# Late exponentials, skip terms as matmul products in PSUM, and PSUM leaving through ScalarE

## The chip, the cores and the metric

The kernel runs on one core of one Trainium2 chip. The metric is the device time of the core in microseconds (us), as the median of several executions. Engines are named as in the profile: PE is TensorE (matrix products), DVE is VectorE, ACT is ScalarE, POOL is GpSimd, SP is SyncE (it issues most transfers).

## The reference, cut to what matters

The kernel computes a sum of three parts over 2048 tokens of 576 channels, and the gradients of all their inputs. The cut version:

```python
xn = layernorm(x)
out = x + ssm_conv(xn, A, B, C, log_dt, Dskip) + ffn(xn, W_gate, W_up, W_down)
# ssm_conv: K[d, l] = Re sum_n C * exp(dt*A*l) * dt*B ;  y = causal_conv(xn, K) + xn * Dskip
# ffn:      (relu(xn @ W_gate) * (xn @ W_up)) @ W_down
# returned: out, and the gradients of x and of all weights for a given grad_out
```

Two places matter. The decay `exp(dt*A*l)` is built from factors that are exponentials of `dt * A_re` times a small set of exponents. And the skip terms `xn * Dskip` (forward) and `grad_out * Dskip` (backward) are added to the two outputs in the last part of the kernel.

## The kernel before

The feed-forward work (matrix products, 11 full chunks of it and a final one) runs the whole time on PE. The transform work of the convolution is cut into small steps, which a greedy scheduler puts between those products when the program is built: every step yields a weight, and the order of all instructions on all engines follows from the weights and from estimates of time. So the order within an engine's queue is fixed at build time.

The final chunk goes through 16 tiles of 128 tokens. For each, PE sums in PSUM the inverse transform of the convolution, the residual, the earlier chunks' sum and the last chunk's products. VectorE has made the skip product `f_base` before, and adds it to PSUM (line 1043):

```python
class Final:
    def load(self, t):
        ...
        self.pool = pool("fin3", 3)                      # at t == 0: three buffers of everything
        ...
        xg = self.pool.tile([P, 2, D], BF16, name="f_xg")
        nc.sync.dma_start(xg[:, 0, :], g.xn_dram[:, t, :])
        nc.sync.dma_start(xg[:, 1, :], g.g_v[:, t, :])
        ...
        base = self.pool.tile([P, 2, D], F32, name="f_base")
        nc.vector.tensor_tensor(base[:], xg[:], self.dsk[:]...to_broadcast([P, 2, D]), op=ALU.mult)   # L1024
        return S3, Ct, xt, xg, acc, base
    def begin(self, t):
        for n in range(t, min(t + 3, ST)):               # loads three tiles ahead
            if n not in self.parts:
                self.parts[n] = self.load(n)
        ...
    def take(self, t, i, cols, ps):                      # four times per tile
        base = self.parts[t][5]
        dst = self.o[:, 0, cols] if i == 0 else base[:, 1, cols]
        self.g.nc.vector.tensor_tensor(dst, base[:, i, cols], ps, op=ALU.add)                         # L1043
    def end(self, t):                                    # gradient of the layer norm
        nc.scalar.activation(acc[:, 1, :], dx, ACT.Copy, accum_out=m[:, 0:1])
        nc.vector.scalar_tensor_tensor(acc[:, 0, :], dx, 1.0, xn, ..., accum_out=m[:, 1:2])           # L1055
        ... # two small ones, one more pass, one activation, one addition, two transfers out
```

The exponentials are made early, in 18 double steps, and written to HBM, from where two halves (each half of the channels) of the transform `p2(0)` and `p2(1)` read them:

```python
def ex_step(i):
    ex = exp_.tile([P, 2 * SX, NE], F32, name="exs")
    v.tensor_tensor(ex[:], pw[:, 0, i*SX:(i+2)*SX]..., self.ev[:]..., op=ALU.mult)
    nc.scalar.activation(ex[:], ex[:], ACT.Exp)
    nc.sync.dma_start(self.ex_dram[:, i:i + 2], ...)
...
yield from self.both(self.p1(0, 4, 10.0), 68.0, self.params(pw), 45.0)      # params holds all ex_steps
with ExitStack() as c:
    pools = self.p2_pools(c)
    yield from self.both(self.p2(0, pools, pw), 0.8 * W2, self.p1(1, 2, 3.0), W1)
    yield from self.both(self.p2(1, pools, pw), 0.8 * W2, self.p3(0, 2, 3.0), W3)
yield from self.p3(1, 4, 8.0)
```

Of the kernel before, what the change touches and what calls it, by code (L numbers as in the profile page):

```python
# [2 lines left out]

# [11 lines left out]
P = 128  # L15
# [141 lines left out]
class Ffn:  # L157
# [110 lines left out]
    def outdx(self, c, sg, j, last=None, turns=()):  # L268
        g, nc = self.g, self.g.nc
        t = sg * JS + j  # L270
        js = slice(j * P, (j + 1) * P)
        if last is None:
            o = self.op.tile([P, 2, D], BF16, name="osx")
        else:
            last.begin(t)
        src = self.t_steps(turns)
        Ts = [self.T[(c, sg, ft)] for ft in range(FTC)]
        for which in range(2):
            for hf in range(2):
                hs = slice(hf * DH, (hf + 1) * DH)  # L280
                if which == 0:
                    mms = [(Ts[ft][0], self.wf[:, 0, ft, hs]) for ft in range(FTC)]
                else:
                    mms = [(Ts[ft][1], self.wf[:, 1, ft, hs]) for ft in range(FTC)] + [(Ts[ft][2], self.wf[:, 2, ft, hs]) for ft in range(FTC)]
                mms = [(lt[:, js], rh) for lt, rh in mms]
                if last is not None:
                    mms = last.terms(t, which, hf) + mms
                ps = g.psum_mm.tile([P, 512], F32, name="ps_mm")
                for i, (lt, rh) in enumerate(mms):
                    nc.tensor.matmul(ps[:, :DH], lhsT=lt, rhs=rh, start=(i == 0), stop=(i == len(mms) - 1))  # L290
                if last is None:
                    g.bal.copy(o[:, which, hs], ps[:, :DH], DH)
                else:
                    last.take(t, which, hs, ps[:, :DH])
                next(src, None)
            if which == 0:
                yield FTC * 0.245
        if last is not None:
            last.end(t)
        elif c == 0:  # L300
            nc.gpsimd.dma_start(g.acc_dram[:, t, :, :], o[:])
        else:
            nc.gpsimd.dma_start(g.acc_dram[:, t, :, :], o[:], accum_op=ALU.add)  # L303
        yield FTC * 0.49
# [155 lines left out]
class S4:  # L460
# [84 lines left out]
    def params(self, pw):  # L545
        g, nc, bal = self.g, self.g.nc, self.g.bal
        v = nc.vector
        with ExitStack() as c:
# [14 lines left out]

            def ex_step(i):
                shp = [P, 2 * SX, NE]
                ex = exp_.tile(shp, F32, name="exs")
                v.tensor_tensor(ex[:], pw[:, 0, i * SX:(i + 2) * SX].unsqueeze(2).to_broadcast(shp), self.ev[:].unsqueeze(1).to_broadcast(shp), op=ALU.mult)
                nc.scalar.activation(ex[:], ex[:], ACT.Exp)
                nc.sync.dma_start(self.ex_dram[:, i:i + 2], ex[:].rearrange("p (i d) e -> p i d e", d=SX))
                bal.add(d=1.4, a=1.2)  # L570

            for i in range(0, 8, 2):
                ex_step(i)
                yield 2.0
            p1 = pool.tile([P, D], F32, name="p1")
            p2 = pool.tile([P, D], F32, name="p2")
            v.scalar_tensor_tensor(pw[:, 1, :], Ai, 1.0 / TWO_PI, dt[:], op0=ALU.mult, op1=ALU.mult)
            for j, (y1, y2, op) in enumerate(((Br, Bi, ALU.subtract), (Bi, Br, ALU.add))):
# [5 lines left out]
                yield 2.0  # L584
            for i in range(8, D // SX, 2):
                ex_step(i)
                yield 2.0

# [29 lines left out]
    def mix(self, dst, src):  # L618
        g, nc = self.g, self.g.nc
        for o in range(2):  # L620
            ps = self.ps()
            for i in range(2):
                nc.tensor.matmul(ps[i * 64:(i + 1) * 64, :DH], lhsT=self.FM[:, o, :], rhs=src[:, i, :], start=True, stop=True)
            g.bal.copy(dst[:, o, :], ps[:, :DH], DH)
            if o == 0:
                yield 0.15

# [35 lines left out]
    def p1(self, hf, n, gap):  # L663
# [11 lines left out]
        with ExitStack() as c:  # L675
# [10 lines left out]
            for h in range(ST + 1):  # L686
                old, Z = Z, None
                if h < ST:
                    b = bs.get(h)
                    if h == 0:  # L690
                        yield gap
                    sg = fp.tile([P, 2, 2, DH], BF16, name="s_ug")
                    for i in range(2):
                        yield from self.mix(sg[:, i], b[:, :, i, :])
                        yield 0.15
                    nc.sync.dma_start(self.S[hf][h], sg[:])
                    Z = self.product(fp, pp, sg[:, 1], sg[:, 0], True)
                    yield 0.7
# [27 lines left out]
    def p3(self, hf, n, gap):  # L726
# [13 lines left out]
        with ExitStack() as c:  # L740
# [13 lines left out]
            for h in range(ST + 1):  # L754
                old, Z = Z, None
                if h < ST:
                    b, sg = bs.get(h)
                    if h == 0:
                        yield gap
                    sk = fp.tile([P, 2, DH], BF16, name="s_k")  # L760
                    yield from self.mix(sk[:], b[:, :, 0, :])
                    Z = self.product(zp, pp, sg[:, 0], sk[:], False), self.product(zp, pp, sg[:, 1], sk[:], True)
                    yield 0.7
# [213 lines left out]
    def gen(self):  # L977
# [4 lines left out]
        with ExitStack() as cp:  # L982
# [9 lines left out]
            with ExitStack() as c:  # L992
                pools = self.p2_pools(c)
                yield from self.both(self.p2(0, pools, pw), 0.8 * W2, self.p1(1, 2, 3.0), W1)
                yield from self.both(self.p2(1, pools, pw), 0.8 * W2, self.p3(0, 2, 3.0), W3)
            yield from self.p3(1, 4, 8.0)

class Final:
# [5 lines left out]
    def load(self, t):  # L1004
        g, nc = self.g, self.g.nc
        if t == 0:
            pool = lambda name, bufs: self.ctx.enter_context(g.tc.tile_pool(name=name, bufs=bufs, reuse_waits="tile"))
            self.dsk = pool("fin1", 1).tile([P, D], BF16, name="dsk")
            nc.sync.dma_start(self.dsk[:], self.Dskip.rearrange("(o d) -> o d", o=1).to_broadcast([P, D]))
            self.pool = pool("fin3", 3)  # L1010
# [11 lines left out]
        nc.sync.dma_start(acc[:], g.acc_dram[:, t])  # L1022
        base = self.pool.tile([P, 2, D], F32, name="f_base")
        nc.vector.tensor_tensor(base[:], xg[:], self.dsk[:].unsqueeze(1).to_broadcast([P, 2, D]), op=ALU.mult)  # L1024
        g.bal.add(d=1.2)
        return S3, Ct, xt, xg, acc, base

    def begin(self, t):
        for n in range(t, min(t + 3, ST)):
            if n not in self.parts:  # L1030
                self.parts[n] = self.load(n)
        self.o = self.pool.tile([P, 2, D], BF16, name="f_o")

    def terms(self, t, i, hf):
        S3, Ct, xt, xg, acc, base = self.parts[t]
        cols = slice(hf * DH, (hf + 1) * DH)
        mms = [(S3[:, ri, :], Ct[:, hf, ri, i, :]) for ri in range(2)]
        return mms + [(self.g.ident_bf[:], r) for r in ([xt[:, cols]] if i == 0 else []) + [acc[:, i, cols]]]

    def take(self, t, i, cols, ps):  # L1040
        base = self.parts[t][5]
        dst = self.o[:, 0, cols] if i == 0 else base[:, 1, cols]
        self.g.nc.vector.tensor_tensor(dst, base[:, i, cols], ps, op=ALU.add)  # L1043
        self.g.bal.add(d=0.37)

    def end(self, t):
        g, nc = self.g, self.g.nc
        S3, Ct, xt, xg, acc, base = self.parts[t]
        o = self.o
        inv_d = 1.0 / D  # L1050
        xn, gt, dx = xg[:, 0, :], xg[:, 1, :], base[:, 1, :]
        nc.sync.dma_start(g.out0_v[:, t, :], o[:, 0, :])
        m = self.pool.tile([P, 4], F32, name="f_m")
        nc.scalar.activation(acc[:, 1, :], dx, ACT.Copy, accum_out=m[:, 0:1])
        nc.vector.scalar_tensor_tensor(acc[:, 0, :], dx, 1.0, xn, op0=ALU.mult, op1=ALU.mult, accum_out=m[:, 1:2])  # L1055
        nc.vector.tensor_scalar(m[:, 2:3], m[:, 1:2], -inv_d, None, op0=ALU.mult)
        nc.vector.tensor_scalar(m[:, 3:4], m[:, 0:1], -inv_d, g.rinv[:, t:t + 1], op0=ALU.mult, op1=ALU.mult)
        nc.vector.scalar_tensor_tensor(dx, xn, m[:, 2:3], dx, op0=ALU.mult, op1=ALU.add)  # L1058
        nc.scalar.activation(dx, dx, ACT.Identity, scale=g.rinv[:, t:t + 1], bias=m[:, 3:4])
        nc.vector.tensor_tensor(o[:, 1, :], dx, gt, op=ALU.add)  # L1060
        nc.sync.dma_start(g.out1_v[:, t, :], o[:, 1, :])
        g.bal.add(d=2.5, a=1.1)

@with_exitstack
def kernel(
# [3 lines left out]
    A_log_dt: bass.AP,  # L1069
    A_Dskip: bass.AP,  # L1070
    grad_out: bass.AP,
# [40 lines left out]
    ffn = Ffn(g, ctx, Wd_in, Wf_in, out_10, out_11, out_12)  # L1112
    s4 = S4(g, par_in, A_log_dt, outs, A_Dskip)
    lnctx, fctx = ExitStack(), ExitStack()
# [10 lines left out]

    final = Final(g, s4, A_Dskip, fctx)
    sgen = s4.gen()
# [22 lines left out]

_INS = ['A_u', 'A_log_dt', 'A_Dskip', 'grad_out', 'gT', 'gq', 'Wd', 'Wf', 'par']
_OUTS = [((1, 2048, 576), 'bfloat16'), ((1, 2048, 576), 'bfloat16'), ((128, 576), 'bfloat16'), ((128, 576), 'bfloat16'), ((128, 576), 'bfloat16'), ((128, 576), 'bfloat16'), ((128, 576), 'bfloat16'), ((128, 576), 'bfloat16'), ((576,), 'bfloat16'), ((576,), 'bfloat16'), ((576, 4608), 'bfloat16'), ((576, 4608), 'bfloat16'), ((4608, 576), 'bfloat16')]

def lay_out(np, inputs):
# [5 lines left out]
    o["gT"] = gT.reshape(NSG, NK, P, JS * P).transpose(0, 2, 1, 3)  # L1160
    o["gq"] = gr.reshape(P, ST, 4, 144).transpose(2, 0, 1, 3)
    g, u, dn = inputs["B_W_gate"], inputs["B_W_up"], inputs["B_W_down"]
    wd = zeros(3, DP, F)
# [36 lines left out]
```

## Time and profile before

| | before |
|---|---|
| median, us (6 runs, range) | 1853.19 (1845.33 to 1858.18) |
| span of the profiled execution | 1851.7 |
| PE busy | 1744.3 (94%) |
| VectorE / ScalarE busy | 1378.7 / 1173.1 |

The page's first part gives the busy time of each engine and its share of the span; of the second part, forty equal slices of the span with the busy share in tenths, these two rows are PE and VectorE.

```profile
PE 1744.3 (94%) x16257; PEld 1182.4 (64%) x16257; DVE 1378.7 (74%) x3223; ACT 1173.1 (63%) x2647; POOL 206.5 (11%) x246
...
PE   7989989999999999999999999999999998899888
...
DVE  7565875786897787777887889889888758824772
```

PE bounds the kernel: a gain must come from the 107 us in which it is idle, or from stretches at a lower clock. PE has gaps at the beginning and in the last seven slices.

The next view is the table of stretches: length, busy time of each engine (with the number of instructions), granted clock, share of DMA time, GB/s. The stretches are cut at marks that every version of the kernel has: the first product of the weight gradient in each chunk, and the first product of the final tiles. In order they are: start to chunk 0; chunk 0 to chunk 1; chunk 4 to chunk 5; chunk 9 to chunk 10 (the third stage of the transform); the final tiles. Chunks are counted from zero (some of the expectations count from one).

```profile
0.00:125.20 125.20, 107.89 (x819) 71.41 (x820) 84.95 (x232) 86.15 (x179) 16.73 (x46) 0.96 0.84 286
125.20:297.50 172.30, 156.41 (x1202) 97.01 (x1200) 120.12 (x291) 115.34 (x267) 15.38 (x18) 0.97 0.92 288
743.40:885.60 142.20, 140.42 (x1488) 99.94 (x1486) 108.52 (x227) 96.13 (x207) 21.41 (x22) 1.00 0.71 183
1474.20:1644.50 170.30, 150.75 (x1185) 93.48 (x1183) 111.31 (x329) 99.67 (x259) 13.84 (x16) 1.00 0.84 234
1695.30:1811.30 116.00, 102.06 (x756) 70.54 (x754) 91.26 (x200) 47.53 (x92) 0.00 (x0) 0.96 0.66 206
```

Length less PE's busy time is PE's idle time: 13.9 us of 116.0 in the final tiles.

Who keeps PE waiting in the final tiles is in the view of waits (engine, line, what it waited for, us in total, times, longest), here first for PE and then for VectorE, in the window of the final tiles.

```profile
PE pt L264 <- DVE dgT L253: 6.6, 3, 2.8
PE ps_mm L290 <- DVE f_o L1043: 5.9, 4, 2.7
PE ps_mm L290 <- DVE f_base L1043: 1.1, 1, 1.1
...
DVE f_base L1024 <- DMA f_xg<-in_grad_out_dram: 14.1, 8, 2.5
DVE f_base L1043 <- PE ps_mm L290: 5.0, 10, 0.7
```

PE waits for VectorE, and VectorE waits for a transfer. One instance in the timeline of VectorE (start, duration, line, operation, operands; in brackets the idle time before it) shows that these are the same wait:

```profile
1743.04 1.36 DVE L1024 TENSOR_TENSOR f_base<-f_xg,dsk 128x1152 f32<-128x1152 bf16 x1 [2.35 <-DMA f_xg<-in_grad_out_dram]
1744.31 0.42 DVE L253 TENSOR_TENSOR dgT<-dhb,upm 128x512 bf16<-128x512 bf16 x1
1744.65 0.42 DVE L255 TENSOR_TENSOR duT<-dhb,rg 128x512 bf16<-128x512 bf16 x1
1744.98 0.81 DVE L1043 TENSOR_TENSOR f_o<-f_base,ps_mm 128x288 bf16<-128x288 f32 x2
```

And the timeline of PE at the same time:

```profile
1742.29 0.53 PE L290 MATMUL ps_mm<-wf,duT 128*128 128x288 bf16 x3
1745.48 0.64 PE L290 MATMUL ps_mm<-bC_28650,S_28648 128*128 128x288 bf16 x2 [2.66 <-DVE f_o L1043]
1745.92 0.44 PE L290 MATMUL ps_mm<-f_acc,ident_bf 128*128 128x288 bf16 x1
1746.16 0.92 PE L290 MATMUL ps_mm<-wf,dgT 128*128 128x288 bf16 x3
```

VectorE stood still from 1740.7 to 1743.0 for data of a later tile, with the addition that frees PE's PSUM buffer behind it in its queue. PE then lost 2.66 us, and afterwards another 1.5 us or so: its products of 288 columns start 240 ns apart from about 1745.5 to 1748.6, where they started 122 ns apart before (the trace records a granted clock of 0.50 from 1745.3 to 1748.7 us).

### The profile page before, as it was taken

What the parts mean: (1) busy time and instruction counts of PE and PEld (TensorE: products, weight loads), DVE (VectorE), ACT (ScalarE), POOL (GpSimd) and SP (SyncE); (2) the same over time, 40 slices, a digit from 0 to 9 for tenths busy, and PEclk for the clock granted to TensorE, in tenths of its full rate; (3) what the DMA queues carried; (4) which work ended last, traced back from release to release, by engine and by line L of the source; (5) the groups of instructions that cost most, each with busy time, mean ns of one, the idle gap of its engine ahead of it and who ended that gap; (6) DMA issues with size and microseconds to landing.
All of it is one profiled execution on the core that took longest, in us unless ns stands there. A gap on an engine that the chain in (4) does not pass through costs nothing. (4 is left out here: it accounts for less than half of the span.)

```text
span 1851.7 us, 41883 instructions
## 1 busy us (share of the span) xinstructions
PE 1744.3 (94%) x16257; PEld 1182.4 (64%) x16257; DVE 1378.7 (74%) x3223; ACT 1173.1 (63%) x2647; POOL 206.5 (11%) x246
## 2 busy tenths in 40 slices
PE   7989989999999999999999999999999998899888
PEld 5665547667666666766666766766766764476566
DVE  7565875786897787777887889889888758824772
ACT  5865865686587488477387567657748746732432
POOL 0200002111012012002102101101201100010000
PEclk9989999999999999999999999999999999999999
DMA  8798988668567576766676756856754779775763
GB/s 284 265 328 295 330 240 265 196 175 232 172 129 207 182 177 170 213 182 156 182 203 150 228 149 160 242 150 123 201 180 85 192 236 274 207 198 181 238 187 101
DMA packets 236411, 373.26 MB, mean 202 GB/s; under 512 B 49202, under 2 KB 153140, under 8 KB 234676
## 3 DMA queue, kind: packets, MB, share of 16 engines
q1 hardware_dynamic: 210244, 304.08, 50.6%
q0 software_dynamic: 24384, 51.92, 18.4%
q10 hardware_dynamic: 1584, 14.60, 2.3%
q8 instruction: 127, 2.08, 0.5%
q14 instruction: 72, 0.59, 0.1%
HBM read 233.08 MB, written 137.43 MB: 200 GB/s over the span
## 5 line engine op out<-in xcount | busy, mean ns | idle before, releaser
L67 ACT CAST osx<-ps_mm 128x288 bf16<-128x288 f32 x684 | 261.7, 423 | 73.9 <-PE ps_mm L290 62.4
L303 POOL DMA_DIRECT2D acc_dram<-osx x160 | 139.7, 877 | 1035.2 <-ACT osx L67 586.3
L290 PE MATMUL ps_mm<-wf,dgT 128*128 128x288 bf16 x1152 | 209.3, 288 | 16.5 <-ACT osx L67 11.5
L290 PE MATMUL ps_mm<-wf,duT 128*128 128x288 bf16 x1152 | 207.7, 288 | 0.0
L343 PEld LDWEIGHTS <-rows 128*128 128x128 bf16 x1536 | 146.0, 98 | 96.2 <-issue 3.6
L290 PE MATMUL ps_mm<-wf,hT 128*128 128x288 bf16 x1152 | 186.3, 288 | 8.2 <-ACT osx L67 2.2
L235 PE MATMUL ps_mm<-xT,wd_158 128*128 128x512 bf16 x720 | 182.4, 379 | 0.7 <-ACT xT L149 0.7
L235 PE MATMUL ps_mm<-xT,wd_159 128*128 128x512 bf16 x720 | 180.7, 379 | 0.6 <-ACT obw L67 0.6
L235 PE MATMUL ps_mm<-gT,wd_160 128*128 128x512 bf16 x705 | 179.7, 381 | 1.2 <-ACT obw L67 1.2
L245 DVE SCALAR_TENSOR_TENSOR upm<-rg,ps_mm 128x512 bf16<-128x512 bf16 x144 | 98.2, 682 | 99.1 <-PE ps_mm L235 71.4
L327 PE MATMUL ps_mm<-rows,hN 128*128 128x144 bf16 x2304 | 157.8, 227 | 0.0
L327 PEld LDWEIGHTS <-hN 128*128 128x128 bf16 x2304 | 148.7, 99 | 7.7 <-issue 5.1
L290 PEld LDWEIGHTS <-dgT 128*128 128x128 bf16 x1152 | 109.7, 98 | 52.9 <-issue 24.7
L343 PE MATMUL ps_mm<-duN,rows 128*128 128x384 bf16 x768 | 138.6, 326 | 0.3 <-DVE upm L245 0.3
L343 PE MATMUL ps_mm<-dgN,rows 128*128 128x384 bf16 x768 | 136.6, 326 | 0.0
L290 PEld LDWEIGHTS <-hT 128*128 128x128 bf16 x1152 | 107.7, 98 | 42.0 <-issue 12.1
L290 PEld LDWEIGHTS <-duT 128*128 128x128 bf16 x1152 | 113.2, 98 | 32.1 <-issue 2.3
L67 ACT CAST obw<-ps_mm 128x384 bf16<-128x384 f32 x105 | 50.1, 477 | 126.4 <-PE ps_mm L343 86.8
L67 ACT CAST dhb<-ps_mm 128x512 bf16<-128x512 f32 x141 | 83.8, 595 | 64.5 <-PE ps_mm L235 62.8
L901 DVE TENSOR_REDUCE Sm<-pr 128x8 f32<-128x256 f32 x288 | 119.2, 414 | 3.6
L243 ACT ACTIVATE rg<-ps_mm 128x512 bf16<-128x512 f32 x144 | 86.8, 603 | 54.4 <-PE ps_mm L235 52.4
L235 PEld LDWEIGHTS <-wd_159 128*128 128x128 bf16 x720 | 65.4, 98 | 62.4 <-issue 2.4
(2513 smaller groups left out, 3515.5 us busy)
## 6 DMA issues: line engine op xcount, KB each, us to landing
acc_dram<-osx POOLq DMA_DIRECT2D x176, 288.0 KB, 4.7
gT<-in_gT_dram SPq DMA_DIRECT2D x48, 640.0 KB, 6.5
xT<-xT_dram SPq DMA_DIRECT2D x44, 640.0 KB, 5.9
rows<-in_gq_dram SPq DMA_DIRECT2D x48, 576.0 KB, 4.3
wf<-in_Wf_dram ACTq DMA_DIRECT2D x11, 1296.0 KB, 8.9
ex_dram<-exs SPq DMA_DIRECT2D x18, 640.0 KB, 5.7
ex<-ex_dram SPq DMA_DIRECT2D x36, 320.0 KB, 3.5
out_dram<-obw SPq DMA_DIRECT2D x96, 96.0 KB, 2.7
```

Source lines behind the costliest of these rows:

```text
L67: self.nc.scalar.copy(out, in_)
L235: nc.tensor.matmul(ps[:], lhsT=w[:, k, fs], rhs=rhs[:, k, :], start=(k == 0), stop=(k == NK - 1))
L243: nc.scalar.activation(rg[:], ps_g[:], ACT.Relu)
L245: nc.vector.scalar_tensor_tensor(upm[:], rg[:], 0.0, ps_u[:], op0=ALU.is_gt, op1=ALU.mult)
L290: nc.tensor.matmul(ps[:, :DH], lhsT=lt, rhs=rh, start=(i == 0), stop=(i == len(mms) - 1))
L303: nc.gpsimd.dma_start(g.acc_dram[:, t, :, :], o[:], accum_op=ALU.add)
L327: nc.tensor.matmul(ps[:, ft * 144:(ft + 1) * 144], lhsT=self.hN[:, st, ft * P:(ft + 1) * P], rhs=gq[:, st, :], start=(st == 0), stop=(st = ...
L343: nc.tensor.matmul(ps[:, :Fc], lhsT=xs[:, st, 0:P], rhs=src[:, st, :], start=(st == 0), stop=(st == ST - 1))
L901: nc.vector.tensor_reduce(out=Sm[:, vi, s0 + dd:s0 + dd + DG, :], in_=pr[:], op=ALU.add, axis=AX.X)
```

## The change

Its intent, part by part:

1. **Final tiles.** The skip terms become 12 more products per tile, of the transposed input (or gradient) with a diagonal matrix of the skip weights, summed in PSUM with everything else. The product on VectorE (L1024) goes, and the sums leave PSUM mostly on ScalarE, which in passing also forms the row sums that the gradient of the layer norm needs.
2. **Exponentials.** Steps of half the size; those for the second half of the channels are made only just before `p2(1)` needs them, at about 800 to 890 us.
3. **Mixing.** In the transform's mixing both products are issued, then both copies (before: product, copy, product, copy).

```diff
@@ feed-forward, final chunk
-                if last is not None:
-                    mms = last.terms(t, which, hf) + mms
+                if last is not None:
+                    src0 = self.X[(c, sg)][which]
+                    mms = [... last.terms(t, which, hf)] + [(src0[:, k, js], last.dsk[:, k, a], b) for k, a, b in last.skip(hf)] + mms
@@ params
-            for i in range(8, D // SX, 2):
-                ex_step(i)
-                yield 2.0
+            for i in range(8, DH // SX):
+                self.ex_step(i, exp_, pw)
+                yield 1.0
+    def ex_step(self, i, pool, pw):        # half the size of the old one
+        ...
+    def late_ex(self, pools, pw):
+        for i in range(DH // SX, D // SX):
+            self.ex_step(i, pools[3], pw)
+            yield 1.0
@@ mix
-        for o in range(2):
-            ps = self.ps()
+        pss = [self.ps() for o in range(2)]
+        for o, ps in enumerate(pss):
             ...matmuls...
+        for o, ps in enumerate(pss):
             g.bal.copy(dst[:, o, :], ps[:, :DH], DH)
-            if o == 0:
-                yield 0.15
@@ order of the stages
-                yield from self.both(self.p2(1, pools, pw), 0.8 * W2, self.p3(0, 2, 3.0), W3)
+                yield from self.both(chain(self.late_ex(pools, pw), self.p2(1, pools, pw)), 0.8 * W2, self.p3(0, 2, 3.0), W3)
@@ Final
-        nc.vector.tensor_tensor(base[:], xg[:], self.dsk[:]...to_broadcast([P, 2, D]), op=ALU.mult)
-    def take(self, t, i, cols, ps):
-        self.g.nc.vector.tensor_tensor(dst, base[:, i, cols], ps, op=ALU.add)
+    def take(self, t, i, hf, cols, ps):
+        if i == 0:
+            self.g.bal.copy(self.o[:, 0, cols], ps, DH)
+        else:
+            self.g.nc.scalar.activation(self.dx[:, cols], ps, ACT.Copy, accum_out=self.m[:, hf:hf + 1])
... (the end of a tile loses one activation and is adapted; the host lays the skip weights out as diagonal blocks)
```

## The prediction

> **What bounds the kernel.** TensorE: busy 1744 of 1852 us (94%, part 1 of the page); VectorE 74%, ScalarE 63%. So time can only come from the 107 us in which PE is idle, and from slow-clock stretches. The table of stretches puts the idle PE time in three places the change touches: 95–165 us (PE 60.7 of 70, granted clock 0.90, DMA share 0.94), 1500–1615 us (98.3 of 115, third transform stage), and the final tiles, 1695–1811 us (102.5 of 116.4, clock 0.96).
>
> **Final tiles.** The timeline of VectorE shows the mechanism. Before each tile VectorE runs the skip product f_base<-f_xg,dsk (L1024, 1.36 us), which must wait for the transfer of f_xg (10 waits, 17.5 us). It stands in VectorE's queue ahead of dgT/duT and of the PSUM additions (L1043, 0.45 us each), so PE waits: 6.6 us for dgT, 7.0 us for L1043 (waits of PE). Idle PE is about 14 us. [...] after a 2.66 us wait at 1745 us, three 288-column products take 0.92 us instead of 0.53, and three stretches of 3.4 us at clock 0.5 lie in this stage, which I estimate at 5 us lost.
> - Removed from VectorE per tile: 1.36 + 4 x 0.45 = 3.2 us (of 5.7), and the early wait for f_xg: it is now needed only by the reduction at the tile's end.
> - Added to PE per tile: 12 products of at most 128 columns. 128x128 transposes run at 55 ns each, so 0.66 us, x16 = 10.6 us (estimate), all on the bounding engine.
> - ScalarE per tile: minus 0.68 + 0.19, plus 4 evictions of 0.42 and 2 accumulator reads of 0.19: 1.7 to about 2.9 us, below PE's 4.6 us per tile. VectorE's and ScalarE's queues are in order, but the built order shows no wait ahead of a PSUM release except the last activation behind VectorE's chain (~2 us), which two evictions of the next tile precede.
> Net: -19 + 10.6 + about 3 residual waits = -5 us.
>
> **Exponentials.** 18 double steps (VectorE 1.49, ScalarE 1.27 us, 640 KB written) become 36 half steps; half of them move from 100–200 us to about 870 us, halving 11.8 MB of writes where DMA is near full. The early double steps blocked VectorE 11.0 us on buffers still being written, and PE 2.9 and 3.1 us behind them. Gain there: 4 us (estimate). The late steps have only two buffers; a cycle of 0.75 + 0.65 + about 4 us to landing against roughly 2.7 us of VectorE work per step in the built order gives short blocks of VectorE, 3 us of PE, where PE has none to spare (195.5 of 200 in 700–900 us). Four more table loads at 1.28 us cost only ScalarE. The transform work ends at the same place in PE's order in both kernels, so nothing is dumped before the final tiles.
>
> **Reordered mixing** (both products, then both copies): ±2 us.
>
> **Prediction:** 1853 - 5 - 4 + 3 - 2 = 1845 us; 80% range 1827 to 1860. Chances: faster by over 2% 0.05, within 2% 0.92, slower 0.03.
>
> **Right if:** PE busy rises by about 10 us; L1024's wait is gone; PE waits on dgT and on evictions in the final stage fall below 5 us, its clock rises to 0.99; PE idle in the early stage falls by some us; the final stage gets about 5 us shorter.
>
> **Wrong if:** PE starts to wait for ScalarE's evictions or for transfers of f_acc in the final tiles (no gain, or slower); late steps block VectorE for tens of us (slower); or the two idle stages, early and 1500–1615 us, both shrink because of the new order (faster than predicted).

## The result, and the profile after

| | before | after |
|---|---|---|
| median, us (runs, range) | 1852.52 (20, 1845.33 to 1858.18) | 1853.38 (10, 1844.85 to 1860.17) |
| ratio of fast runs, 95% interval | | 1.0002 [0.9986, 1.0017] |
| span of the profiled execution | 1851.7 | 1850.8 |
| PE busy in it | 1744.3 | 1750.6 |

A ratio here and below is the mean time of one kernel's fast runs over the mean time of the other's of the same rounds, so it is not quite the ratio of the medians quoted beside it. A per cent is 18.5 us. The time lies inside the predicted range, which at 33 us is four times as wide as the forecast gain; the gain of 8 us itself was not there.

The same parts of the page for the kernel after:

```profile
PE 1750.6 (95%) x16449; PEld 1190.1 (64%) x16449; DVE 1342.9 (73%) x3173; ACT 1191.7 (64%) x2722; POOL 205.8 (11%) x246
...
PE   7989989999999999999999999999999998899999
...
DVE  7565976678788788688668899898789746922551
```

The table of stretches, with the same marks:

```profile
0.00:120.90 120.90, 105.38 (x819) 70.54 (x820) 82.67 (x234) 85.25 (x183) 16.67 (x46) 0.99 0.83 281
120.90:299.60 178.70, 160.05 (x1256) 100.06 (x1254) 123.69 (x309) 112.91 (x274) 20.02 (x21) 0.96 0.89 267
745.20:893.30 148.10, 140.43 (x1413) 97.24 (x1411) 116.64 (x241) 105.43 (x220) 21.87 (x22) 1.00 0.73 204
1478.00:1653.10 175.10, 155.08 (x1208) 93.93 (x1206) 109.09 (x331) 100.74 (x260) 13.80 (x16) 0.99 0.82 227
1704.70:1810.50 105.80, 104.48 (x948) 76.95 (x946) 57.30 (x135) 59.67 (x147) 0.00 (x0) 1.00 0.76 239
```

Line by line against before: -4.3, +6.4, +5.9, +4.8 and -10.2 us. The final tiles gained 10.2 us, and nearly all of it had been lost before they began: the final tiles start at 1704.7 instead of 1695.3. (Stages not shown differ by +2.8, -2.3, -0.8, +0.1, -2.9, +0.1, -1.3 and +0.8, and the tail after the final tiles by -0.1. The sum of all is -0.9 us.)

The stretches are cut at marks of the feed-forward work, so they need not hold the same transform work: by the tables the kernel after has 54 more products in the second stretch, 75 fewer in the third and 23 more in the fourth. A difference of length is therefore lost time and moved work together, and PE's idle time (length less busy time) is the cleaner reading. Over all stages but the final tiles, PE's idle time rose by 5.4 us and its busy time by 3.9 us, which together take back 9.3 of the 10.2 us.

In the final tiles, the waits of PE and of VectorE after are:

```profile
PE ps_mm L236 <- DMA gT<-in_gT_dram: 1.1, 1, 1.1
...
DVE f_acc L1070 <- ACT f_dx L1061: 28.5, 14, 4.1
DVE f_o L1075 <- ACT f_dx L1074: 9.0, 12, 1.0
```

VectorE now waits much longer than before, 28.5 us for ScalarE's evictions alone, and it costs nothing: VectorE is busy for 57 of 106 us, and PE waits for it no more. A wait matters only if something that bounds the kernel stands behind it.

Between the fourth and the fifth chunk PE has new idle time, 7.7 us where there were 1.8 us. There its waits are, first before (1.6 us in three waits, the longest shown) and then after (in total 7.3 us, all on VectorE and ScalarE):

```profile
PE pt L264 <- DVE hT L247: 1.2, 1, 1.2
```

```profile
PE ps_mm L292 <- ACT osx L68: 2.2, 3, 0.9
PE ps_mm L292 <- DVE upm L246: 2.0, 3, 1.5
PE ps_mm L292 <- DVE hT L248: 0.8, 1, 0.8
```

They are many small waits, mostly for ordinary feed-forward work (`osx`, `upm`, `hT`), not for the exponentials themselves. (Two of the waits for `osx`, 1.5 us together, do follow an exponential that had stood waiting in ScalarE's queue just before.)

### The profile page after: what moved, and what is told of

The parts are those of the page before. It is cut to its first block, busy times and chain, and to the rows that moved or that the text cites. A ratio compares the mean times of both kernels' runs of the same rounds, so it can differ in the third digit from the quotient of the medians.

```text
span 1850.8 us, 42341 instructions
## 1 busy us (share of the span) xinstructions
PE 1750.6 (95%) x16449; PEld 1190.1 (64%) x16449; DVE 1342.9 (73%) x3173; ACT 1191.7 (64%) x2722; POOL 205.8 (11%) x246
## 5 line engine op out<-in xcount | busy, mean ns | idle before, releaser
L292 PE MATMUL ps_mm<-wf,dgT 128*128 128x288 bf16 x1152 | 208.5, 287 | 20.4 <-ACT osx L68 17.5
```

The lines of the kernel that those rows point to most:

```text
L292: nc.tensor.matmul(ps[:, cs], lhsT=lt, rhs=rh, start=(i == 0), stop=(i == len(mms) - 1))
```

## The experiments

Eighteen kernels ran. "Stage 4-5" is the stretch from the fourth to the fifth chunk, "final" the final tiles, both from the one profiled execution of each run, whose idle times and stage lengths carry its own scatter.

### Which part does what: one part alone

Each of these three is the kernel before with one part of the change (1, 2 or 3 of the list above) taken from the kernel after, unaltered.

```diff
 e1_final_only:  + part 1 (skip terms in PSUM, evictions)
 e2_exp_only:    + part 2 (half steps, second half late)
 e3_mix_only:    + part 3 (both products, then both copies)
```

> The kernel before with only the change of the final tiles (skip products in PSUM, evictions on ScalarE). Theory A (the final tiles gain about 10 us, and the loss of 9 us elsewhere belongs to the exponentials and the reordered mixing): 1841 to 1846 us, ratio about 0.995; the final stage, 116.0 us in the kernel before and 105.8 us in the changed one, takes 105 to 107 us here, with PE idle in it below 3 us, and no stage ahead of it changes by more than 3 us. Rival B (what the final tiles gain is always given back because another order of the earlier stages comes with it): within 3 us of the kernel before, with the earlier stages longer by some 9 us.

> The kernel before with only the change of the exponentials (half-size steps, second half late). Theory A: slower by 5 to 9 us, 1858 to 1861 us; PE idle between the fifth and the sixth weight-gradient stage up by about 6 us as in the changed kernel (7.7 instead of 1.8 us). Rival C (the loss belongs to the reordered mixing): within 3 us of the kernel before.

> The kernel before with only the reordered mixing (both products, then both copies). Theory A: within 3 us of the kernel before. Rival C: slower by 5 to 9 us, with the third transform stage longer by about 5 us as in the changed kernel.

| | ratio to before | median (before 1855.18) | stage 4-5 | third transform stage | final |
|---|---|---|---|---|---|
| e1_final_only | 0.9953 [0.9938, 0.9968] | 1846.35 | 142.2 | 173.6 | 106.2 |
| e2_exp_only | 1.0017 [0.9998, 1.0037] | 1858.02 | 148.6 | 170.1 | 114.0 |
| e3_mix_only | 0.9993 [0.9976, 1.0010] | 1854.13 | 142.2 | 178.4 | 114.3 |

Part 1 alone gains 8.7 us, as expected (theory A). Part 2 alone gains nothing and rather costs: 3 us, fewer than the 5 to 9 that were expected, with an interval that reaches 1. The stage in which its late half runs is 6.4 us longer. Part 3 alone is not to be told from nothing in time, though the third transform stage of its profile is longer.

### Two parts at a time, and two controls

```diff
 c0_before_again:  the kernel before, unaltered
 c1_after_again:   the kernel after, unaltered
 c2_final_mix:     before + parts 1 and 3
 c3_final_exp:     before + parts 1 and 2
```

> The kernel before, unchanged, as a control. Ratio 1.000 within 0.002; its profile shows how far the lengths of single stages vary with no change of code: I expect up to 2 us for most stages and up to 8 us for the stage that holds the third transform, whose length differed by 3 to 8 us in runs that share its code.

> The changed kernel, unchanged, on this chip. Theory D (the three parts add up: -8.7 for the final tiles, +3.2 for the exponentials, -1.3 for the mixing, so -6.8 us): ratio 0.996. Theory I (the parts interact, and together they lose 5 to 7 us more than one by one): ratio 1.000 within 0.0015 as measured before.

> Final tiles and mixing, exponentials as before. Theory D: ratio 0.9945 (-10 us). Theory I with the interaction between these two: ratio 0.998 or more. If the interaction lies between final tiles and exponentials: 0.9945.

> Final tiles and exponentials, mixing as before. Theory D: ratio 0.997 (-5.5 us). Theory I with the interaction between these two: 1.000 or more. If the interaction lies between mixing and exponentials: 0.997.

| | ratio to before | median (before 1851.73) | stage 4-5 | third transform stage | final |
|---|---|---|---|---|---|
| c0_before_again | 0.9984 [0.9961, 1.0007] | 1851.06 | 142.2 | 172.9 | 111.7 |
| c1_after_again | 0.9986 [0.9965, 1.0007] | 1851.54 | 148.8 | 176.1 | 106.7 |
| c2_final_mix | 0.9964 [0.9944, 0.9984] | 1847.26 | 142.2 | 177.6 | 106.2 |
| c3_final_exp | 1.0007 [0.9985, 1.0029] | 1855.13 | 149.3 | 173.1 | 105.3 |

The control says how far to trust all this: the same kernel against itself came out at 0.9984, and its final stage at 111.7 instead of 116.0 us. So a tenth or two of a per cent is not read. What stands out of that noise is that parts 1 and 3 together keep the gain and parts 1 and 2 together lose it. The loss belongs to part 2. By these times it costs more on top of part 1 (10 us) than alone (3 us). c1 and c3 came out nearer to the expectation with such an interaction than to the plain sum, c2 between the two. But the spans of the profiled executions don't show it (5.6 us against 6.7), so it may be scatter; that is open.

Single stages scatter unequally. Stage 4-5 takes 142.2 to 142.4 us in all eleven profiles without the late half. The second stage (chunk 0 to chunk 1) took 169.9 to 176.1 us in profiles in which PE's queue there is the same as before, and the final tiles of the two profiles of the kernel before took 116.0 and 111.7 us.

### Final tiles: was it the wait?

**Taking the wait away (wrong result).** The product no longer reads `f_xg`; it has the same length, place and engine.

```diff
-  nc.vector.tensor_tensor(base[:], xg[:], self.dsk[:]..., op=ALU.mult)
+  nc.vector.tensor_tensor(base[:], self.dsk[:]..., self.dsk[:]..., op=ALU.mult)
```

> Wrong result on purpose: the kernel before, but the skip product multiplies the resident skip weights by themselves instead of the loaded f_xg; same VectorE instruction, 1.36 us, but nothing to wait for. Theory W (PE's idle time in the final stage comes from VectorE waiting for f_xg at the head of its queue): the stage falls from 112 to 116 us to 98 to 104 us, PE idle in it from 14 to below 4 us, ratio 0.992 to 0.995. Rival V (it comes from the amount of VectorE's work there): the stage stays above 110 us.

Measured: 0.9910 [0.9891, 0.9929], 1836.60 us (before 1853.67); final stage 97.1 us with 1.0 us of PE idle. The work of VectorE is all still there. So the final stage before was long because of the wait, not because of the amount of VectorE's work, and the wait is worth more (17 us in time, 18.9 us of the stage) than the change gains in that stage. The stage in the table of stretches, with as much VectorE work as before (89.5 us; before 91.3):

```profile
1696.30:1793.40 97.10, 96.06 (x755) 68.38 (x753) 89.53 (x200) 48.38 (x93) 0.00 (x0) 1.00 0.79 245
```

**Evicting on VectorE instead of ScalarE.** The kernel before with the skip products in PSUM, but with VectorE copying the sums out:

```diff
-  self.g.bal.copy(self.o[:, 0, cols], ps, DH)                       # and ScalarE's accumulating copy
+  self.g.nc.vector.tensor_copy(self.o[:, 0, cols], ps)              # both outputs
```

> Final tiles as in the change, but the sums leave PSUM on VectorE (4 copies of about 0.45 us per tile) and the row sum is taken by a ScalarE pass as before; exponentials and mixing as before. Theory W: the wait is gone all the same, final stage 105 to 109 us, ratio 0.995 to 0.997. Rival E (the eviction on ScalarE is what counts): stage above 111 us, ratio above 0.998.

Measured: 0.9977 [0.9958, 0.9997], 1849.40 us; final stage 105.6 us with 1.2 us idle. That stage is as short as with ScalarE (105.3 to 106.7), so the move of the evictions to ScalarE is not what shortens it. (Whether the whole kernel is slower than e1_final_only, which had 0.9953 in another call, these runs don't settle.)

**Deeper prefetch (a miss).** The kernel before with four buffers and four tiles ahead:

```diff
-            self.pool = pool("fin3", 3)
+            self.pool = pool("fin3", 4)
-        for n in range(t, min(t + 3, ST)):
+        for n in range(t, min(t + 4, ST)):
```

> The kernel before with the final tiles' inputs loaded four tiles ahead instead of three, in four buffers instead of three; no product is moved to PE. If the idle PE time of the final stage comes from VectorE waiting for the late f_xg at the head of its queue, the waits for f_xg (17.5 us) nearly vanish and the final stage falls from 116 us to 99 to 104 us, faster than by the change itself because no PE work is added: 1838 to 1843 us. If it comes from VectorE's amount of work in these tiles (91 of 116 us busy), the stage stays above 110 us and the time within 4 us of the kernel before.

Measured: 0.9997 [0.9978, 1.0015], 1854.38 us; the final stage took 110.5 us, which by the expectation alone would have spoken for the amount of VectorE's work (x_base_nowait refuted that); the waits for `f_xg` in the whole kernel even rose, from 17.5 us (10 times) to 27.1 us (12 times). The expected gain was missed altogether, and the trace says why. The transfer and the product that needs it are issued by the same function, so loading one tile earlier moved both. From the issue of the transfer to the start of the product it took 2.4 to 6.2 us in the kernel before (for 15 of the 16 tiles; median of all 4.6), and 3.2 to 9.6 us (median 4.5) here. In these runs it was not the number of buffers that hid the transfer, but the distance between its issue and its first use (32 us or more for all but the first three tiles of v_xg_ahead below, where VectorE did not wait for `f_xg` in the final tiles).

**The product on GpSimd.**

```diff
-        nc.vector.tensor_tensor(base[:], xg[:], self.dsk[:]..., op=ALU.mult)
-        g.bal.add(d=1.2)                     # the entry in the balance of copies between VectorE and ScalarE
+        nc.gpsimd.tensor_tensor(base[:], xg[:], self.dsk[:]..., op=ALU.mult)
```

> A version meant to beat both: the kernel before with the skip product of the final tiles on GpSimd, which is idle in that stage (an estimate from its 1.67 us for 128x512 elements: 3.8 us for one tile, of 6 us per tile). The wait for f_xg then blocks no other engine's queue and PE gets no work. If that holds: final stage 97 to 101 us, ratio 0.991 to 0.993. If GpSimd is too slow or slows VectorE: above 104 us, ratio above 0.995.

Measured: 0.9978 [0.9961, 0.9996], 1848.42 us (before 1852.97); final stage 108.5 us with 11.0 us idle. The wait for the transfer no longer stands in VectorE's queue, but another one is there. The view of one source line shows VectorE's pass over `f_base` and `f_xg` (min/median/max ns) with the product on VectorE, and then GpSimd's product and the same VectorE pass in the experiment:

```profile
L1055 DVE SCALAR_TENSOR_TENSOR f_acc<-f_base,f_xg x16: 749/757/759, 1699.9 to 1812.1; 128x576 bf16<-128x576 f32 x16
```

```profile
L1024 POOL TENSOR_TENSOR f_base<-f_xg,dsk x16: 2350/2364/2582, 1510.4 to 1797.4; 128x1152 f32<-128x1152 bf16 x16
...
L1054 DVE SCALAR_TENSOR_TENSOR f_acc<-f_base,f_xg x16: 757/757/2481, 1699.4 to 1804.9; 128x576 bf16<-128x576 f32 x16
```

This VectorE pass beside GpSimd's product takes up to 1.7 us longer. It is not alone: in the final tiles nine VectorE passes of five source lines took 1.6 to 2.2 us longer than their median before, 17.9 us in all, and each of the nine overlaps a product on GpSimd. The longest of these delays, 2.2 us, is shorter than one GpSimd product (2.36 us, the median). What holds the passes up was not shown. That these delays explain the remaining idle time of PE was not tested by itself.

**Loading further ahead of the use (correct result).** The prefetch again, now with transfer and product apart: `f_xg` in its own pool of 8 buffers, issued six tiles ahead; the product stays on VectorE, two tiles ahead.

```diff
+            self.xpool, self.xgs = pool("finx", 8), {}
-        xg = self.pool.tile([P, 2, D], BF16, name="f_xg")
-        nc.sync.dma_start(xg[:, 0, :], g.xn_dram[:, t, :])
-        nc.sync.dma_start(xg[:, 1, :], g.g_v[:, t, :])
+        for n in range(t, min(t + 6, ST)):
+            if n not in self.xgs:
+                self.xgs[n] = self.xpool.tile([P, 2, D], BF16, name="f_xg")
+                nc.sync.dma_start(self.xgs[n][:, 0, :], g.xn_dram[:, n, :])
+                nc.sync.dma_start(self.xgs[n][:, 1, :], g.g_v[:, n, :])
+        xg = self.xgs[t]
```

> Correct result wanted: the kernel before, whose f_xg (the operand of the skip product) lies in a pool of its own with 8 buffers and is loaded six tiles ahead, not with the rest; the product stays on VectorE. Wait theory: if the data are there early enough, the wait for f_xg goes, the final stage falls from 112-116 to 97-102 us (the run without the wait had 97) and the ratio is 0.991 to 0.994. Rival, from the run with deeper pools: the order of the instructions follows the estimated arrival of the data, so the product is moved up again to meet them and waits as before; final stage 110 or more, ratio about 1.000.

Measured: 0.9934 [0.9921, 0.9946], 1840.61 us (before 1852.66), as expected. From issue to use there are now 32 us or more for every tile but the first three. The table of stretches for its final tiles, and the waits of PE there:

```profile
1700.00:1797.20 97.20, 95.69 (x748) 68.36 (x753) 89.56 (x200) 48.44 (x93) 0.00 (x0) 1.00 0.74 230
```

```profile
PE ps_mm L290 <- DVE f_o L1048: 0.5, 1, 0.5
PE pt L264 <- ACT hN L67: 0.3, 1, 0.3
```

The stage takes 97.2 us at a granted clock of 1.00, with 1.5 us of PE idle: the same as without the wait, and VectorE works as much as before. This is 12 us faster than the kernel before, and by the ratios about as much faster than the kernel after. It is the fastest correct version here; its lead over part 1 alone (0.9953) is 3.5 us by the ratios, about as large as their intervals, and 9 us by the final stage.

### Exponentials: what does the late half cost?

**Half steps, all early.** Part 1 with the steps halved, but none moved.

```diff
-            for i in range(8, DH // SX):
+            for i in range(8, D // SX):        # and no late_ex; no part 3
                 self.ex_step(i, exp_, pw)
```

> Final tiles as in the change, exponentials in half-size steps but all of them early; mixing as before. If the loss comes from the late half: the stage between the fifth and sixth weight-gradient phase is back from 148 to 149 us to 142 us, the first two stages together take 296 to 300 us, ratio 0.995 to 0.997. If it comes from the half-size steps: 1.000.

Measured: 0.9959 [0.9939, 0.9979], 1846.84 us (before 1853.67); stage 4-5 at 142.2 us. The halving costs nothing that shows (e1 had 0.9953); the move to late does. Against c3_final_exp (1.0007), which differs only in the move, that is 0.5 per cent or 9 us, across two calls.

The next five take one thing out of the late steps of the kernel after, or move it. All but x_late_pool give a wrong result (the second half of the transform then reads the first half's values, or garbage). In x_late_empty the steps' entries in the balance of copies between VectorE and ScalarE went with them.

```diff
 x_late_noexp:    late steps:  - nc.scalar.activation(ex[:], ex[:], ACT.Exp)
 x_late_nowrite:  late steps:  - nc.sync.dma_start(self.ex_dram[:, i], ex[:])
 x_late_noprod:   late steps:  - nc.vector.tensor_tensor(ex[:], ...);  the exponential reads its factor directly
 x_late_pool:     late steps:  - nc.vector.tensor_tensor(...)  + nc.gpsimd.tensor_tensor(...)
 x_late_empty:    late_ex:     - self.ex_step(i, pools[3], pw);  its 18 turns `yield 1.0` stay
```

> Wrong result on purpose: the changed kernel without the Exp activation in the late steps (and so without the four table loads that go with it); the VectorE products and the writes stay. If ScalarE's queue is the cause of the late loss (Exp waits there for VectorE, with evictions behind it): the stage between the fifth and sixth weight-gradient phase falls from 148 to 149 us to 142 to 144 us. If buffers still being written or VectorE's work are the cause: it stays at 147 us or more. Nothing is expected of the whole time, one look.

> Wrong result on purpose: the changed kernel, whose late steps do not write their result out (the second half then reads the first half's values), so the two late buffers come free when Exp has ended; VectorE's products and ScalarE's Exp stay. If VectorE's waits for buffers still being written (8 to 9 us in all four profiles with late steps, none before) cause the late loss: the stage between the fifth and sixth weight-gradient phase falls from 148 to 149 us to 142 to 144 us. If the 18 products and Exps in that place are the cause by their work and order alone: 147 us or more.

> Wrong result on purpose: the kernel after, whose late steps have no product on VectorE (the exponential reads its factor directly); exponentials and writes stay. If VectorE's products are what PE waits behind, the stage from the fourth to the fifth chunk falls to 142-144 us; if 147 or more, the product alone is not it.

> The changed kernel with the late products on GpSimd instead of VectorE, correct result. The buffer waits then stand in GpSimd's queue, which no eviction shares. If VectorE is the carrier of the late loss (its waits or its added work): 142 to 145 us in that stage, ratio 0.996 to 0.998. If ScalarE or the table loads carry it: 147 us or more, ratio as the changed kernel, 0.998 to 1.000.

> Wrong result on purpose: the kernel after, whose second half of exponentials is not computed at all, while the generator keeps its 18 turns of weight 1.0 (the second half of the transform reads the first half's values). Theory A, the steps' own work in the queues costs: the stage from the fourth to the fifth chunk falls from 148-149 to 142-144 us, ratio near 0.996. Theory B, the 18 turns shift the transform's later work against the products: stage stays at 147 or more, ratio near 1.000.

| | time, us (ratio to before) | stage 4-5 (PE idle in it) |
|---|---|---|
| before (for comparison) | 1852.52 | 142.2 (1.8) |
| after (for comparison) | 1853.38 (1.0002) | 148.1 (7.7) |
| x_late_noexp | 1864.81, one run, state unknown | 153.2 (11.2) |
| x_late_nowrite | 1856.95, one run, state unknown | 149.1 (9.2) |
| x_late_noprod | 1867.22, one run, state unknown | 156.5 (15.5) |
| x_late_pool | 1868.72 (1.0075 [1.0050, 1.0100]) | 162.7 (17.3) |
| x_late_empty | 1848.97 (0.9976 [0.9961, 0.9992]) | 146.5 (7.1) |

The times of x_late_noexp, x_late_noprod and x_late_pool can't be put down to their late steps alone. Their second stage took 186 to 189 us (the kernel after: 178.7), some 500 us before the first late step, though the queues of all engines have the same order as in the kernel after up to there. Only stage 4-5 is read. (Where product records are missing from a trace, as in the last four rows but not in x_late_noexp, idle time reads a little high: the kernel after has 7.7 us there, its repetition with such gaps 9.0.)

Three theories of a sole carrier fall here. Not the writes and the buffers that they hold: without writes VectorE's waits of 8.0 us for a buffer still being written are gone (2.2 us are left, for ScalarE), and the stage stayed at 149. Not ScalarE's time alone: without the exponential the stage is not shorter. Not VectorE's time alone: without the product, it is longer by 8 us. That removing work makes a stage longer has one plain reading: it does not act through the amount of work alone, but through where the rest comes to stand and wait. The waits of ScalarE in x_late_noprod and in x_late_pool show where:

```profile
ACT ex L591 <- DMA ex_dram<-ex: 9.7, 5, 3.7
```

```profile
ACT ex L589 <- POOL ex L588: 15.7, 12, 4.3
```

Without the product, the wait for a buffer still being written moved from VectorE's queue to ScalarE's; with the product on GpSimd, ScalarE waits for GpSimd. The evictions that PE needs stand behind. PE's waits for ScalarE in this stage rose from 3.0 us in the kernel after to 11.0 and 11.8 us. In x_late_noprod, 8.0 of the 11.0 us are five waits that each follow, within 3 us, an exponential that had itself waited 1.1 to 3.7 us. In x_late_noexp PE waited once 5.5 us for `upm`: VectorE was not waiting then but busy with passes of the transform that stand ahead of `upm` in its queue; why they came to stand there, the runs don't say. So these are not clean removals: the order of VectorE's and ScalarE's queues in this stage changed with each of them (of ScalarE's 219 instructions in the kernel after, 202 keep theirs in x_late_nowrite and 181 in x_late_noprod).

The last run carries most of the verdict on this stage. With no step at all, only its 18 turns in the scheduler, the stage still has 146.5 us, 4.3 of the 5.9 us that the change lost there, and its PE waits are of the same kind as after:

```profile
748.00:894.50 146.50, 139.44 (x1398) 97.39 (x1409) 107.75 (x231) 91.97 (x197) 22.36 (x22) 0.99 0.69 179
```

```profile
PE ps_mm L292 <- DVE upm L246: 3.4, 3, 1.5
PE ps_mm L292 <- ACT osx L68: 1.3, 3, 0.9
PE ps_s L890 <- ACT dk L68: 0.8, 1, 0.8
```

This is half a microsecond under what its expectation had asked of theory B (147 or more) and far from theory A (142 to 144), so most of the loss in this stage is the order's, not the steps'.

To see the order itself, we took PE's products in this stage out of each trace, as a list of names without buffer numbers, and counted the longest sequence that two kernels have in common, in order. From before to e1, e3 and x_half_early all 1484 keep it (in some other traces 12 records are missing, and the rest keep it); the stage has 142.2 us in all of them. From before to after only 1030 of 1484 and 1411 do; about a quarter of what PE does in this stage after the change is interleaved otherwise or is other work. From after to x_late_empty, which has none of the work, 1354 of 1411 do. In every profile with the late turns, 95 per cent or more of the queue is that of after, and the stage takes 146.5 us or more (nine, the kernel after and its repetition among them); in every one without them the queue is that of before, and it takes 142.2 to 142.4 us (eleven, with the kernel before and its control).

What is not settled is how the whole loss divides between the order and the steps. In stage 4-5, x_late_empty wins back 1.6 of 5.9 us. But that stage is not the whole: the stages around it give some back. The eight stages from chunk 1 to chunk 9 together take 1174.4 us in c2_final_mix (no late half), 1175.1 in x_late_empty and 1178.3 and 1178.8 in the kernel after and its repetition, so over this longer stretch the order alone costs little and the steps the larger part. By the times x_late_empty stands at 0.9976, between c2_final_mix (0.9964) and after (1.0002, in its repetition 0.9986), which points the same way. These are single profiles; the same eight stages scatter from 1175.7 to 1179.9 us in profiles without parts 2 and 3, and the control moved by 0.16 per cent.

## Why the prediction was right or wrong, point by point

- **"TensorE bounds, so time can only come from its idle time and slow-clock stretches."** Right. Every gain and loss that was traced above is PE's idle time, its work or its clock, and VectorE's 28.5 us of new waits in the final tiles cost nothing.
- **Final tiles: "-19 + 10.6 + about 3 residual waits = -5 us."** The mechanism was right: x_base_nowait removed only the wait, and the stage fell from 116.0 to 97.1 us, by the 19 us predicted. Two sizes were off. Residual waits were put at 3 us; PE is idle for 1.3 us after. The products were put at 55 ns each, as if all had 128 columns; only half of them do. They start 56, 43 and 28 ns apart for 128, 96 and at most 64 columns, which is 0.53 us for the 12 of a tile and 8.5 us in all, not 10.6. The stage gained 10.2 us in the profile, and part 1 alone 8.7 us in time.
- **Exponentials, early: "Gain there: 4 us (estimate)."** Wrong. The first stage became 4.3 us shorter, and the next one 6.4 us longer: net +2.1 us. Its assumption was that half the steps give half the trouble. But VectorE's waits for a step's buffer between 95 and 200 us went only from 11.0 to 9.6 us. And the turns that were taken out let the transform's work move up: the second stage holds 54 more products (3.6 us of PE's busy time). In e2 and c3 it is longer too (180.8 and 179.2 us; 172.3 before). Both stages together take 299.6 to 300.7 us in the four profiles with part 2 unaltered (e2, c3, the kernel after and its repetition), and 294.9 to 302.0 us in the eleven without the late half, so what can be said is that the gain of 4 us did not appear, not that 2 us were lost.
- **Exponentials, late: "short blocks of VectorE, 3 us of PE, where PE has none to spare."** This is the step that failed, together with the early gain. The blocks came as foretold (8.0 us of VectorE, four waits), but they are not the carrier, for x_late_nowrite took them away and the stage did not shrink (149.1 us). In their place, the runs show the new order of PE's own queue: 18 more turns ahead of `p2(1)` shift its work against the feed-forward products, and that stage gets 5.9 us longer, all of it idle time of PE; 4.3 us stay when the steps do nothing at all (x_late_empty). The prediction checked that the transform "ends at the same place in PE's order" and took it that nothing else moves; between its beginning and end, only 1030 of 1411 products of that stage keep their order. In time, part 2 costs 3 us alone and 10 us on top of part 1, where -1 us (-4 + 3) was predicted. That the late half costs this is shown (x_half_early against c3_final_exp, and c2_final_mix against c3_final_exp); how much of it over the whole kernel is the order and how much the steps is open.
- **Mixing: "±2 us"**, counted as -2. A gain of 2 us is not shown. It measured -0.07 per cent alone and +0.11 per cent on top of part 1, both within noise. The nine profiles with part 3 have a third transform stage of 174.2 to 178.4 us, the eleven without it 170.0 to 173.6; in turn the eight stages from chunk 1 to chunk 9 are shorter with it (1174.4 us in c2 and 1172.3 in e3, against 1175.7 to 1179.9 without parts 2 and 3). Part of this is work moved from one stage to another, so the net stays open.
- **The sum.** With stages from the profile: -10.2 (final tiles) + 2.1 (early) + 5.9 (late) = -2.2, and 1.3 us over all other stages (4.8 in the third transform stage, the rest gives back); measured -0.9 us of span. In time the kernels are equal.
- **"Right if":** PE's busy time rose by 6.3 us rather than 10. L1024 and its wait are gone, PE's waits in the final stage fell to 1.1 us, and its clock rose to 1.00, all as foretold. Early idle time did not fall: with 17.3 + 15.9 us before and 15.5 + 18.6 us after in the first two stages, it rose by 0.9 us.

## What to carry to other kernels

When an engine that bounds a kernel waits for another, look in that other engine's queue for what stands ahead of the instruction it needs; here it was a transfer's wait, and issuing the transfer earlier, apart from its use, gained 12 us with no new work, where moving the arithmetic to the bounding engine gained 9. A deeper pool that moved the load and its first use together hid nothing here (27.1 us of waits with four buffers, 17.5 us with three). Where a scheduler decides the order, a step that is moved costs, beside its own work, what the new order does to the bounding engine's queue: compare that queue over its whole length, not only where it ends, and read an experiment that deletes work with the same care, for it moves the rest as well.

## Clock, spacing and waits as the traces show them

- In the kernel before, the trace records a granted clock of 0.50 in stretches that begin at 106.9, 137.6, 270.7, 1267.4, 1642.9, 1745.3, 1762.3 and 1796.5 us; the first lasts 10.2 us, the third 6.8 us and each of the others 3.4 us. (One more, from 1851.1 us, lies after the last product.) Each of the eight begins in a wait of PE of 2.5 to 5.5 us, or up to 1.6 us after its end. In the 3.4 us before the three in the final tiles PE was idle for 2.4, 2.4 and 2.2 us. What sets the clock back was not shown.
- The recorded stretches and the spacing of the products agree: after the wait from 1742.8 to 1745.5 us, products of 288 columns started 240 ns apart instead of 122 ns, for about 3 us, and the stretches recorded at 1745.3, 1762.3 and 1796.5 us are where the slow products stand (from about 1745.5, 1762.4 and 1796.6 us).
- In sustained streams at a granted clock of 1.00, products started 56 ns apart for 128 columns, 122 for 288 and 216 for 512 (kernel before), and 43 for 96 (kernel after).
- Transposes of 128x128 on PE started 55 to 56 ns apart, and 107 ns apart in a stretch at a granted clock of 0.50, so they do follow the clock. Their records are 0.22 us long each, and overlap.
- Distance from the issue of `f_xg` to its first use: with about 4.6 us (median), three buffers left 17.5 us of waits, and with 4.5 us four left 27.1 us; with 32 us or more there were none in the final tiles.
